# A gated mix of a state-space scan and linear attention: input loads and the order of all four engines set anew

## The chip, the cores and the metric

The kernel runs on one core of one Trainium2 chip. TensorE (PE) multiplies matrices and writes to PSUM; VectorE (DVE) and ScalarE (ACT) read PSUM and work on SBUF; GpSimd (POOL) prepares masks here; SyncE (SP) issues most of the transfers. ScalarE's and GpSimd's own queues issue some as well. The metric is the device time of one execution in microseconds (us).

## The reference, cut to what matters

```python
x = A_x                                                   # [1, 2048, 512], bf16
g = sigmoid((x * gate_w).sum(-1, keepdims=True))
# a: a diagonal complex state space of 512 states
Lam_bar = exp(dt * Lam);  B_bar = ((Lam_bar - 1) / Lam)[:, None] * Bmat
h[t] = Lam_bar * h[t-1] + x[t] @ B_bar.T
a = 2 * real(h @ Cmat.T) + x * Dskip
# b: linear attention, 32 heads of 16, with a softmax feature map of both signs
q, k, v = split(x @ wqkv)
phi(u) = concat(softmax(u @ w_phi), softmax(-u @ w_phi))
kv = sum_s phi(k)[s] v[s];  z = sum_s phi(k)[s]
b = ((phi(q) @ kv) / (phi(q) @ z + 1e-6)) @ wo
return g * a + (1 - g) * b
```

## The kernel before, in words

The 2048 rows of x are taken in four interleaved sets f = 0 to 3 (row 4r + f), each of 512. So four steps of the recurrence become one step of a scan over 512 places, and the rows between are filled in afterwards. All the work is bf16 matmuls with 128 partitions of contraction.

A function `_fast_path` does the whole computation. Behind it stands a general path, which runs only if a flag, loaded at the end, says that some value was too large for the fast one.

*Loads* (L310 to L324, L332). These are emitted ahead of everything else, so each queue issues them in program order. SP: two halves of `xn` (set 0 of x, rows on partitions, L311); three transposing loads of `xT` for sets 1 to 3 (L315); two transposing loads of `BT`, the real and imaginary parts of B (L319); `Wc` (L320); transposed `Wk` and `Wq` (L321, L322); `Wo` in four parts (L324). ScalarE's queue: `Wv` in two halves (L313), then five short vectors into `vec_n` (L317), of 1 KB each. GpSimd's queue: three short vectors in another layout into `vq` (L332). [...]

*Start.* Six matmuls on zeros (L415) come first on PE. Then PE transposes the four 128-row chunks of `xn` (L426, four 128-wide transposes each; chunks 0 and 1 need its first half, 2 and 3 its second), and ScalarE (L371) or DVE (L373) copies each from PSUM to `xT`. The V tiles (L443) are 16 units of 4 matmuls each, `Wv` being the moving operand; the first unit is a task of two matmuls (contraction parts 0 and 1, `Wv` first half) and a task of two more. Their results go to `vx` on ScalarE. The small transposes (L478, L480, L483) bring the short vectors onto partitions; after them DVE and ScalarE compute the discretised state-space parameters, which the gate, the tables for the scan and the diagonal matrices `dgL`, `dgS` and `Dd` need.

*Middle.* `g_unit` (L670, L675) multiplies x by B for each set and adds the term of the recurrence from the set before; results go to `Gs`. `scan_unit` (L708 to L726) runs the scan on DVE. `k_unit` (L782 to L813) and `q_unit` (L870) make the exponentials of the features, their sums and the state `KVbd`; `fold` (L650) multiplies `Wk` and `Wq` with `w_phi` beforehand. `fill_unit` (L750 to L758) on DVE adds the scan's carry to the sets 0, 1 and 2: its last product, L758, finishes a piece of `Gs`. The small softmax sums (L948 and around) are DVE's too.

*End.* `mix` does one block of 128 output rows at a time, 16 in all: attention numerators (L979), their evacuation (L982) and scaling (L986), the state-space output (L995, reading `Gs` and the transposed C, `CT`), a transposing transfer (L1003), the product with `Wo` added to the same PSUM bank (L1011), the evacuation with the gate's factor (L1016 on ScalarE, L1018 on DVE) and the store (L1022). The last block is evacuated and stored in two halves of 256 columns, and the flag is transposed, tested and loaded beside it.

*What sets the order.* A small planner, `_Plan` (L44 on), holds every piece of work as a task with a cost for each engine that can do it. The tuple `ORDER` (L172 on) lists all tasks in the order in which they are emitted: each entry is twice the task's number, plus one if the second of its engines takes it. Each engine so runs its tasks in the order of the list. Loads appear in the planner only as due times (`pl.at`, L378 to L379), which with the tasks' costs decide which PSUM bank a task gets: a task takes the bank that the planner thinks free first, from the groups A (four), B (two) and C (two). No due time holds an instruction up by itself; what waits on the chip are the semaphores.

Of the kernel before, what the change touches and what calls it, by code (L numbers as in the profile page):

```python
# [12 lines left out]
ACT = mybir.ActivationFunctionType  # L13
# [5 lines left out]
P = 128  # L19
# [103 lines left out]
def kernel(  # L123
# [34 lines left out]
    Pst = A_Lambda_re.shape[0]  # L158
    assert D == 512 and Pst == 512 and H * Dh == D and Dh == 16 and S == 2048
    flag_i = _fast_path(tc, A_x, A_Lambda_re, A_Lambda_im, A_B_re, A_B_im, A_C_re, A_C_im, A_log_dt, A_Dskip,  # L160
                        B_wqkv, B_w_phi, B_wo, gate_w, out)
    with tc.If(flag_i != 0, label="general"):
# [4 lines left out]
F = 4  # L167
# [2 lines left out]
GATE_LIMIT = 60.0  # L170
NWARM = 6
ORDER = (  # L172
    8, 10, 14, 18, 13, 22, 21, 156, 16, 190, 24, 266, 174, 268, 0, 26, 28, 4, 32, 162, 30, 192, 34, 158, 176, 36,
    40, 166, 2, 38, 132, 164, 42, 198, 44, 134, 46, 61, 760, 138, 53, 79, 194, 202, 196, 168, 758, 77, 55, 160,
    764, 81, 186, 67, 170, 762, 200, 182, 57, 136, 766, 154, 84, 378, 140, 172, 204, 188, 142, 144, 380, 382, 91,
    502, 178, 392, 64, 384, 63, 294, 88, 184, 286, 180, 504, 96, 288, 70, 398, 386, 282, 148, 59, 68, 73, 150,
    290, 297, 394, 292, 506, 146, 285, 388, 390, 152, 509, 75, 336, 338, 330, 298, 332, 48, 397, 404, 406, 400,
    334, 340, 83, 304, 50, 302, 86, 409, 418, 308, 306, 438, 300, 442, 444, 448, 410, 342, 344, 362, 403, 420,
    510, 346, 512, 440, 310, 348, 312, 446, 314, 450, 516, 316, 452, 422, 412, 522, 350, 352, 518, 320, 364, 454,
    354, 6, 322, 414, 424, 476, 562, 456, 514, 356, 324, 460, 462, 470, 100, 326, 98, 524, 520, 464, 416, 102,  # L180
    328, 534, 426, 526, 480, 528, 474, 358, 478, 530, 360, 466, 542, 104, 532, 472, 544, 108, 428, 546, 566, 206,
    458, 568, 548, 106, 220, 210, 430, 564, 536, 572, 482, 570, 110, 214, 318, 538, 370, 208, 372, 484, 600, 432,
    216, 574, 486, 112, 488, 212, 576, 492, 434, 226, 218, 578, 594, 494, 222, 114, 468, 496, 116, 540, 224, 238,
    228, 626, 550, 230, 498, 118, 232, 604, 234, 628, 552, 634, 246, 598, 236, 248, 580, 240, 120, 436, 602, 596,
    92, 630, 554, 250, 366, 582, 640, 252, 242, 122, 584, 586, 636, 632, 606, 556, 588, 374, 124, 768, 376, 244,
    490, 686, 642, 724, 126, 608, 500, 644, 638, 646, 726, 718, 128, 652, 590, 610, 94, 254, 728, 592, 648, 692,
    720, 368, 654, 690, 650, 696, 688, 656, 774, 658, 722, 660, 694, 666, 1210, 662, 668, 612, 270, 256, 778, 558,
    258, 1214, 780, 698, 614, 700, 702, 616, 730, 704, 670, 708, 776, 260, 618, 130, 278, 810, 710, 732, 664, 712,
    734, 620, 272, 280, 1212, 274, 798, 792, 812, 276, 672, 784, 736, 740, 674, 816, 782, 742, 802, 262, 622, 814,
    840, 624, 714, 794, 676, 716, 560, 786, 842, 744, 746, 800, 748, 834, 678, 818, 820, 804, 790, 844, 788, 796,  # L190
    808, 1204, 754, 756, 750, 828, 264, 752, 848, 846, 836, 852, 806, 850, 832, 854, 822, 856, 1208, 830, 1206,
    680, 1216, 682, 948, 944, 884, 858, 862, 864, 826, 878, 824, 838, 866, 860, 868, 946, 902, 950, 952, 880, 870,
    1062, 1036, 954, 956, 1222, 1010, 1002, 958, 706, 1220, 1076, 1218, 1004, 872, 1006, 996, 1048, 1078, 1074,
    998, 1028, 1054, 684, 1050, 960, 1056, 1012, 1000, 1052, 1030, 976, 1008, 1032, 962, 1058, 1022, 874, 1024,
    1224, 1026, 978, 964, 970, 1064, 1014, 972, 1038, 984, 1060, 1080, 1034, 980, 1226, 974, 966, 986, 982, 968,
    1184, 770, 1178, 1180, 1232, 1040, 876, 886, 1016, 1234, 1100, 882, 1082, 904, 890, 1186, 1084, 1018, 1102,
    1228, 988, 1042, 1158, 1160, 1182, 1188, 892, 1190, 894, 1086, 1114, 1152, 1230, 1154, 1066, 1068, 1106, 1156,
    1090, 1162, 1070, 1132, 1104, 1196, 990, 1192, 1092, 1072, 1164, 1094, 888, 1044, 1096, 1108, 1166, 992, 1046,
    1194, 1110, 1098, 1170, 1126, 1134, 1260, 908, 1136, 1254, 1236, 1128, 1116, 1112, 1168, 896, 1130, 738, 898,
    1198, 1172, 1262, 1280, 1238, 1118, 1138, 1264, 1200, 1256, 994, 1140, 1240, 914, 1244, 900, 906, 1020, 1312,  # L200
    1144, 1142, 1282, 1174, 1246, 1258, 916, 1314, 1248, 1306, 1120, 1286, 1268, 1266, 1272, 1146, 1308, 1288,
    1316, 1284, 1346, 1148, 1310, 1332, 1177, 918, 1338, 910, 1250, 1318, 1340, 912, 1202, 1334, 1290, 1294, 1252,
    920, 1324, 1296, 1390, 1392, 1242, 1270, 1122, 1088, 1336, 1292, 922, 926, 1342, 1274, 1384, 1276, 1386, 924,
    1320, 1364, 1358, 1298, 1360, 1322, 1151, 928, 1348, 1326, 1436, 1366, 1344, 932, 930, 1300, 1424, 1394, 938,
    1388, 940, 1302, 1328, 1362, 1350, 1410, 1125, 1396, 1352, 1442, 1416, 934, 942, 1398, 1330, 936, 1372, 1400,
    1412, 1368, 1374, 1418, 1370, 1420, 1414, 1422, 1402, 1404, 1444, 1376, 1438, 1354, 1426, 1446, 1440, 1428,
    1279, 1357, 772, 1448, 1305, 1468, 1406, 1450, 1452, 1378, 1454, 1430, 1380, 1408, 1382, 1470, 1472, 1456,
    1462, 1459, 1432, 1434, 1465, 1461, 1466)
KR = 0
GR = 0  # L210
ENGINES = {mybir.EngineType.PE, mybir.EngineType.DVE, mybir.EngineType.Activation, mybir.EngineType.Pool}
# [2 lines left out]
def _pe(n, cols):  # L214
    return {"PE": n * max(30.0, cols / 2.4 + 3.0)}
# [11 lines left out]
def _fast_path(ctx, tc, A_x, A_Lambda_re, A_Lambda_im, A_B_re, A_B_im, A_C_re, A_C_im, A_log_dt, A_Dskip,  # L227
               B_wqkv, B_w_phi, B_wo, gate_w, out):
    nc = tc.nc
    S, D, H, Dh, Pst = 2048, 512, 32, 16, 512  # L230
# [14 lines left out]
    def ctile(shape, dt, name):  # L245
        return const.tile(shape, dt, name=name)
# [10 lines left out]
    Wv = ctile([P, KT, D], BF16, "Wv")  # L257
# [29 lines left out]
    vec_n = ctile([20, P], BF16, "vec_n")  # L287
# [10 lines left out]
    xn = wk.tile([P, F, D], BF16, tag="ET0", name="xn", bufs=1)  # L298
# [8 lines left out]
    nc.scalar.preload_act_table_set(ACT_SET)  # L307
    vsrc = (A_log_dt, A_Lambda_re, A_Lambda_im, A_Dskip, gate_w)
    x0 = xf[0].rearrange("(a c) d -> c a d", c=P)
    for h in range(2):  # L310
        nc.sync.dma_start(out=xn[:, 2 * h:2 * h + 2], in_=x0[:, 2 * h:2 * h + 2])  # L311
    for k in (0, 2):
        nc.scalar.dma_start(out=Wv[:, k:k + 2, :], in_=B_wqkv[k * P:(k + 2) * P, 2 * D:3 * D].rearrange("(k p) n -> p k n", p=P))  # L313
    for f in range(1, F):
        nc.sync.dma_start_transpose(out=xT[:, :, f * NCH:(f + 1) * NCH], in_=xf[f])  # L315
    for n, src in enumerate(vsrc):
        nc.scalar.dma_start(out=vec_n[4 * n:4 * n + 4, :], in_=src.rearrange("(j p) -> j p", p=P))  # L317
    for ri, B_ in enumerate((A_B_re, A_B_im)):
        nc.sync.dma_start_transpose(out=BT[:, :, ri, :], in_=B_)  # L319
    nc.sync.dma_start(out=Wc[:], in_=B_w_phi.rearrange("(k hl) e f -> (hl e) k f", hl=8))  # L320
    nc.sync.dma_start_transpose(out=WkT, in_=B_wqkv[:, D:2 * D])  # L321
    nc.sync.dma_start_transpose(out=WqT, in_=B_wqkv[:, 0:D])  # L322
# [7 lines left out]
    nc.gpsimd.memset(KVbd[:], 0.0)  # L330
    for n in range(3):
        nc.gpsimd.dma_start(out=vq[:, n, :], in_=vsrc[n].rearrange("(q t) -> q t", t=2 * NT))  # L332
    nc.vector.memset(eps_t[:], 1e-6)
    nc.vector.memset(hpi_t[:], float(np.pi / 2.0))
    nc.vector.memset(sg[0:64, :], 1.0)
# [3 lines left out]
    nc.vector.memset(selq[:], 0.0)  # L339
    nc.vector.memset(vx[:, :, :, Dh:Dh + 1], 1.0)  # L340

    pl = _Plan({"DVE": 2.4e3, "ACT": 5.0e3, "PE": 1.1e3, "SP": 26.0e3})

    def psum(prefix):
        def make(k):
# [28 lines left out]
        return pl.add(cost, fn, deps=deps, bufs=[b] + list(bufs), rank=rank)  # L374

    A1 = ("A", "B")
    d_x = [pl.at(t) for t in (4.1, 4.9, 7.7, 10.2, 12.7)]
    d_wv0, d_wv, d_b, d_wk, d_wq, d_wo = (pl.at(t) for t in (4.9, 5.7, 18.0, 21.0, 23.3, 26.0))  # L378
    d_vec, d_wc = pl.at(8.5), pl.at(18.5)  # L379

    def tcols(f, a):
        return slice(f * NCH + a * P, f * NCH + (a + 1) * P)
# [38 lines left out]
    for a in range(4):  # L421
# [5 lines left out]
        t = pl.add({"PE": 460.0} if a < 2 else _pe(4, 128), tr, deps=[d_x[a // 2]], follow=[t_warm], bufs=[b, early[0]])  # L427
# [1249 lines left out]
```

## Time and profile before

Device time in four runs: 154.40, 154.03, 154.10 and 153.65 us, median 154.07.

| | |
|---|---|
| profiled execution, its own time | 154.53 us |
| its span | 152.4 us |
| mean granted clock of PE | 0.993 |
| busy: PE, DVE, ACT, POOL | 145.1, 129.1, 110.1, 4.3 us |
| PE matmuls | 1124 |
| moved by the DMA engines | 14.95 MB, 98 GB/s in the mean |
| landings: `xn` halves, `Wv` halves | 4.11, 5.57; 4.67, 6.19 us |
| landings: `xT` sets 1, 2, 3; `BT` | 9.62, 10.47, 13.84; 16.0, 17.9 us |

Times inside the execution count from the start of its span. In the profile, a row of slices gives the busy share of each fortieth of the span in tenths. A row of the timeline gives the start, the length, the engine (PEld is PE's weight load, SPq, ACTq and POOLq are queues of transfers), the line of the kernel, the operation, what it writes and reads, the shape, how many instructions stand in the row, and in brackets how long the engine had been idle before and what ended that.

### The profile page before, as it was taken

The page shows a single profiled execution, that of the slowest core. Times are in us where ns is not written, and L with a number is a line of the kernel's source. Part 1 is how long each engine was busy: PE and PEld are TensorE (multiplying, and loading weights), DVE is VectorE, ACT ScalarE, POOL GpSimd, SP SyncE. Part 2 cuts the span into 40 slices and gives each one's busy share as a digit, 9 for nine tenths or more (in the row PEclk, how much of TensorE's full clock was granted, in tenths as well). Part 3 has the DMA queues.
Part 4 walks back from the last instruction along what each step waited for, and adds up shares of the span by engine and source line. Part 5 has one row for each costly group of instructions (what it writes and reads, how often), then busy time and mean ns, then how long its engine had stood idle before and what let it go on. Part 6 is the DMA issues. An engine that isn't in the chain of part 4 may idle for free.

```text
span 152.4 us, 3179 instructions
## 1 busy us (share of the span) xinstructions
PE 145.1 (95%) x1124; PEld 83.8 (55%) x1124; DVE 129.1 (85%) x370; ACT 110.1 (72%) x221; POOL 4.3 (3%) x14
## 2 busy tenths in 40 slices
PE   6899999999999999999999999999999999999950
PEld 1535566555566656655545565756555556555720
DVE  2407999799999999999799999999999999998030
ACT  3217898998888898989999999877784756263130
POOL 8200000000000000000000000000000000000000
PEclk9999999999999999999999999999999999999997
DMA  3969998900112323434133213033744141227330
GB/s 112 312 144 271 171 210 210 234 8 0 34 34 69 73 69 103 106 89 52 34 86 103 97 49 103 22 69 69 73 105 104 35 103 39 69 69 201 77 92 24
DMA packets 37211, 14.95 MB, mean 98 GB/s; under 512 B 29384, under 2 KB 37192, under 8 KB 37192
## 3 DMA queue, kind: packets, MB, share of 16 engines
q1 hardware_dynamic: 35504, 13.33, 39.9%
q10 hardware_dynamic: 1592, 1.38, 2.8%
q8 instruction: 10, 0.16, 0.5%
q14 instruction: 9, 0.07, 0.2%
q0 software_dynamic: 96, 0.00, 0.0%
HBM read 1.60 MB, written 2.10 MB: 24 GB/s over the span
## 4 chain that ended last, share of the span: by engine, by line


## 5 line engine op out<-in xcount | busy, mean ns | idle before, releaser
L670 PE MATMUL pp<-xT,BT 128*128 128x512 bf16 x128 | 32.0, 380 | 0.0
L995 PE MATMUL pp<-CT,Gs 128*128 128x512 bf16 (+1 forms) x104 | 23.7, 363 | 0.0
L670 PEld LDWEIGHTS <-BT 128*128 128x128 bf16 x128 | 17.8, 145 | 8.9
L982 ACT CAST late<-pp 128x512 bf16<-128x512 f32 x32 | 17.9, 589 | 5.8 <-PE pp L979 5.8
L1016 ACT ACTIVATE late<-pp,Gg 128x512 bf16<-128x512 f32 x15 | 10.3, 691 | 13.6 <-PE pp L1011 10.9
L240 ACT ACTIVATE E<-pp 128x512 bf16<-128x512 f32 x32 | 17.6, 606 | 1.3 <-PE pp L782 0.6
L240 ACT ACTIVATE ET<-pp 128x512 bf16<-128x512 f32 x32 | 17.3, 617 | 0.7 <-PE pp L870 0.6
L443 PE MATMUL pp<-Wv,xT 128*128 128x512 bf16 x64 | 17.3, 416 | 0.0
L1011 PE MATMUL pp<-Wo,late 128*128 128x512 bf16 (+1 forms) x68 | 16.1, 366 | 0.0
L782 PE MATMUL pp<-Wk,xT 128*128 128x512 bf16 x64 | 15.6, 379 | 0.0
L870 PE MATMUL pp<-xT,Wq 128*128 128x512 bf16 x64 | 15.4, 379 | 0.0
L995 PEld LDWEIGHTS <-Gs 128*128 128x128 bf16 x104 | 9.6, 98 | 7.5
L986 DVE TENSOR_TENSOR late<-late 128x512 bf16<-128x512 bf16 x32 | 13.0, 434 | 0.0
L371 ACT CAST Gs<-pp 128x512 bf16<-128x512 f32 x20 | 11.7, 591 | 1.6 <-PE pp L675 1.6
L371 ACT CAST vx<-pp 128x512 bf16<-128x512 f32 x16 | 8.8, 602 | 4.4 <-PE pp L443 4.3
L979 PE MATMUL pp<-KVbd,ET 128*128 128x128 bf16 x128 | 10.7, 219 | 0.1
L443 PEld LDWEIGHTS <-xT 128*128 128x128 bf16 x64 | 6.5, 107 | 7.8 <-issue 2.4
L979 PEld LDWEIGHTS <-ET 128*128 128x128 bf16 x128 | 8.5, 98 | 3.4 <-DVE qmax L949 0.3
L782 PEld LDWEIGHTS <-xT 128*128 128x128 bf16 x64 | 6.2, 98 | 6.8
L806 DVE TENSOR_TENSOR E<-E,rc 128x2048 bf16<-128x2048 bf16 x8 | 9.6, 1221 | 0.0
L870 PEld LDWEIGHTS <-Wq 128*128 128x128 bf16 x64 | 6.0, 98 | 6.6
L718 DVE TENSOR_TENSOR_SCAN c<-sp,c 128x512 bf16<-128x512 f32 x8 | 9.4, 1216 | 0.0
(170 smaller groups left out, 242.4 us busy)
## 6 DMA issues: line engine op xcount, KB each, us to landing
Zs<-c SPq DMA_DIRECT2D x32, 64.0 KB, 2.1
out_dram<-late SPq DMA_DIRECT2D x9, 128.0 KB, 2.1
c<-c SPq DMA_DIRECT2D x16, 64.0 KB, 2.0
CT<-ET SPq DMA_DIRECT2D x8, 128.0 KB, 3.1
out_dram<-late ACTq DMA_DIRECT2D x6, 128.0 KB, 1.9
xn<-in_A_x_dram SPq DMA_DIRECT2D x2, 256.0 KB
Wv<-in_B_wqkv_dram ACTq DMA_DIRECT2D x2, 256.0 KB, 4.9
Wo<-in_B_wo_dram SPq DMA_DIRECT2D x4, 128.0 KB, 2.8
```

Source lines behind the costliest of these rows:

```text
L240: return nc.scalar.activation(**kw)
L371: nc.scalar.copy(out=o, in_=view(b))
L443: MM(out=f32v(b), lhsT=xT[:, kt, tcols(f, a)], rhs=Wv[:, kt, :], start=(kt == 0), stop=(kt == KT - 1))
L670: MM(out=f32v(b), lhsT=BT[:, kt].rearrange("p r (q t) -> p (r q) t", t=NT)[:, :, j + 4 * h], rhs=xT[:, kt, f * NCH:(f + 1) * NCH], start=( ...
L782: MM(out=f32v(b), lhsT=xT[:, kt, tcols(f, a)], rhs=Wk2[:, kt, :], start=(kt == 0), stop=(kt == KT - 1))
L870: MM(out=f32v(b), lhsT=Wq2[:, kt, g * P:(g + 1) * P], rhs=xT[:, kt, f * NCH:(f + 1) * NCH], start=(kt == 0), stop=(kt == KT - 1))
L979: MM(out=f32v(pn[sgn])[:, g * P:(g + 1) * P], lhsT=ets[f].t[:, sgn, g, cs], rhs=KVbd[:, sgn, g, :], start=True, stop=True)
L982: tn = pl.add(_act(512), lambda e, sgn=sgn: nc.scalar.copy(out=o2.t[:, sgn], in_=f32v(pn[sgn])), deps=[t], bufs=[pn[sgn], o2], rank=rank + 2)
L986: VT(out=v, in0=v, in1=als[f].t[:, a, sgn * H:(sgn + 1) * H].rearrange("p (g h) -> p g h", g=HG).unsqueeze(2).to_broadcast([P, HG, Dh, 8]) ...
L995: MM(out=f32v(py)[:, 0:w], lhsT=st, rhs=CT[:, tt // 2 + 4 * (tt % 2), n * w:n * w + w], start=(tt == 0), stop=False)
L1011: MM(out=f32v(py)[:, 0:w], lhsT=oT.t[:, g, :], rhs=Wo[:, g, hs], start=False, stop=(g == HG - 1))
L1016: nc.scalar.mul(out=ot.t[:, hs], in_=f32v(py)[:, 0:w], mul=Gg[:, ti:ti + 1])
```

## The change

The loads are emitted in another order. The second half of `Wv` moves from ScalarE's queue to SP, between the halves of `xn`; the third `xT` moves behind both parts of `BT`; the fourth and fifth short vectors of `vec_n` move from ScalarE's to GpSimd's queue, behind `vq`. The due times are written anew, and the whole of `ORDER` is replaced, for all engines. The shapes and the number of PE's instructions stay as they are. Some tasks go to the other engine: `Gs` evacuations on DVE are 6 in place of 4 (18 on ScalarE in place of 20), those of `Wk` 1 in place of 2, those of `xT` 3 in place of 2. On PE the list now begins with the warm-up matmuls, the transposes of chunks 0 and 1, the first two matmuls of V (entry 156), the transposes of chunks 2 and 3 (18 and 22), and then the rest of V; before, entry 156 stood behind 22. After V of set 0 and the small transposes, V tiles of sets 1 and 2 and three of the gate's units come ahead of the work on `BT`, and what reads the third set of x comes at the 27th PE task or later.

```diff
 ORDER = (
-    8, 10, 14, 18, 13, 22, 21, 156, 16, 190, 24, 266, 174, 268, 0, 26, 28, 4, 32, 162, 30, 192, 34, 158, 176, 36,
...
+    8, 10, 13, 14, 156, 18, 17, 22, 2, 174, 158, 20, 25, 266, 160, 4, 190, 0, 26, 28, 270, 194, 192, 30, 32, 176,
...
-    for h in range(2):
-        nc.sync.dma_start(out=xn[:, 2 * h:2 * h + 2], in_=x0[:, 2 * h:2 * h + 2])
-    for k in (0, 2):
-        nc.scalar.dma_start(out=Wv[:, k:k + 2, :], in_=B_wqkv[k * P:(k + 2) * P, 2 * D:3 * D].rearrange("(k p) n -> p k n", p=P))
-    for f in range(1, F):
+    nc.sync.dma_start(out=xn[:, 0:2], in_=x0[:, 0:2])
+    for k, q in ((0, nc.scalar), (2, nc.sync)):
+        q.dma_start(out=Wv[:, k:k + 2, :], in_=B_wqkv[k * P:(k + 2) * P, 2 * D:3 * D].rearrange("(k p) n -> p k n", p=P))
+    nc.sync.dma_start(out=xn[:, 2:4], in_=x0[:, 2:4])
+
+    def xload(f):
         nc.sync.dma_start_transpose(out=xT[:, :, f * NCH:(f + 1) * NCH], in_=xf[f])
-    for n, src in enumerate(vsrc):
-        nc.scalar.dma_start(out=vec_n[4 * n:4 * n + 4, :], in_=src.rearrange("(j p) -> j p", p=P))
+    xload(1)
+    xload(2)
     for ri, B_ in enumerate((A_B_re, A_B_im)):
         nc.sync.dma_start_transpose(out=BT[:, :, ri, :], in_=B_)
+    for n in range(3):
+        nc.scalar.dma_start(out=vec_n[4 * n:4 * n + 4, :], in_=vsrc[n].rearrange("(j p) -> j p", p=P))
+    xload(3)
...
     for n in range(3):
         nc.gpsimd.dma_start(out=vq[:, n, :], in_=vsrc[n].rearrange("(q t) -> q t", t=2 * NT))
+    for n in range(3, 5):
+        nc.gpsimd.dma_start(out=vec_n[4 * n:4 * n + 4, :], in_=vsrc[n].rearrange("(j p) -> j p", p=P))
...
-    pl = _Plan({"DVE": 2.4e3, "ACT": 5.0e3, "PE": 1.1e3, "SP": 26.0e3})
+    pl = _Plan({"DVE": 2.4e3, "ACT": 5.6e3, "PE": 1.1e3, "SP": 27.0e3})
...
-    d_x = [pl.at(t) for t in (4.1, 4.9, 7.7, 10.2, 12.7)]
-    d_wv0, d_wv, d_b, d_wk, d_wq, d_wo = (pl.at(t) for t in (4.9, 5.7, 18.0, 21.0, 23.3, 26.0))
-    d_vec, d_wc = pl.at(8.5), pl.at(18.5)
+    d_x = [pl.at(t) for t in (4.1, 6.2, 9.2, 11.4, 19.5)]
+    d_wv0, d_wv, d_b, d_wk, d_wq, d_wo = (pl.at(t) for t in (4.8, 5.6, 17.0, 22.7, 24.8, 27.0))
+    d_vec, d_wc = pl.at(9.5), pl.at(20.5)
```

## The prediction

> **What bounds the kernel now.** I read the page's busy shares first, then its slices, then busy time by stretches, then the order of time at the start, then the waits.
>
> ```profile
> PE 145.1 (95%) x1124; PEld 83.8 (55%) x1124; DVE 129.1 (85%) x370; ACT 110.1 (72%) x221; POOL 4.3 (3%) x14
> PE   6899999999999999999999999999999999999950
> DVE  2407999799999999999799999999999999998030
> ```
>
> TensorE (PE) is the bound: 145.1 of 152.4 us. Its slices are full from the third to the 38th. VectorE (DVE) is nearly as full from the fourth on, and the average of 85% hides this: what it lacks lies in the first 12 us and the last 12.
>
> ```profile
> 4.20:6.40 2.20, 1.78 (x16) 1.52 (x17) 0.56 (x2) 0.17 (x1) 0.75 (x2) 1.00 1.16 332
> 6.40:11.50 5.10, 5.10 (x17) 1.85 (x14) 0.79 (x7) 1.50 (x3) 0.00 (x0) 1.00 0.81 172
> ...
> 30.00:70.00 40.00, 40.00 (x266) 24.07 (x265) 39.64 (x102) 35.94 (x75) 0.00 (x0) 1.00 0.27 63
> 70.00:100.00 30.00, 29.88 (x288) 17.11 (x286) 28.91 (x71) 28.24 (x63) 0.00 (x0) 1.00 0.21 64
> 100.00:140.00 40.00, 40.00 (x330) 22.99 (x327) 39.90 (x114) 24.60 (x48) 0.00 (x0) 1.00 0.40 83
> 140.00:152.40 12.40, 7.02 (x54) 4.34 (x51) 1.86 (x9) 2.07 (x3) 0.00 (x0) 0.92 0.31 79
> ```
>
> After each stretch come its length and the busy time of PE, weight loads, DVE, ACT and POOL (instructions in brackets), then granted clock, DMA share and GB/s. From 30 to 140 us PE is busy 109.88 of 110 us: no matmul there can start earlier unless one before it does. So only about 11 us at the start and 5 at the end can give time back. DVE is busy 39.90 of the 40 us before 140, so in that stretch every microsecond of DVE work added or started late comes out somewhere.
>
> ```profile
> 1.27 2.74 PE L415 MATMUL pp<-warm 128*128 128x512 bf16 x6 [1.27 <-DVE warm L306]
> ...
> 4.16 1.03 PE L426 MATMUL pp<-ident,xn 128*128 128x128 bf16 x8
> ...
> 5.61 1.04 PE L426 MATMUL pp<-ident,xn 128*128 128x128 bf16 x8 [0.42 <-DMA xn<-in_A_x_dram]
> ...
> 6.44 5.17 PE L443 MATMUL pp<-Wv,xT 128*128 128x512 bf16 x14
> ...
> 11.55 0.18 PE L478 MATMUL pp<-ident,vec_n 20*128 20x20 bf16 x1
> ```
>
> Columns: start, length, engine, line. Four transposes of x need a chunk of `xn` each; the second half of `xn` landed at 5.57, so PE stood from about 5.0 to 5.61. The 14 matmuls of V began at 6.44. They start 0.427 us apart until 10.45, and 0.216 apart afterwards: the clock was low for the first ten.
>
> ```profile
> ACT xT L371 <- PE pp L426: 4.1, 1, 4.1
> ACT vx L371 <- PE pp L443: 3.5, 1, 3.5
> ```
>
> [...]
>
> **The change, part by part.** (1) *First two V matmuls into the gap.* Each of the two input issues on SP took 0.49 us (0.98 for two, from 0.74). The order on SP becomes `xn` first half at 0.74, `Wv` second half at 1.23, `xn` second half at 1.72, with `Wv` first half on ScalarE's queue at 0.86 as before. The four 256 KB loads landed at 4.11, 4.67, 5.57 and 6.19 in the order of their issue; the second half of `xn` goes from third to fourth, so I take 6.19 for it (ends: 5.57, if queues share the engines so that its place is kept; 6.5, if it comes behind more of SP's work). PE then does: transposes 4.16 to 5.0; the first evacuation, 4.81 to 5.23 in the row of DVE; two V matmuls from about 5.30, 2 x 0.427 = 0.85, to 6.15; transposes from 6.23 (landing plus 0.04, as 5.57 to 5.61) to 7.06 (8 x 0.107, less the overlap at the end). Before, the transposes ended at 6.44; two V matmuls after them ended at 7.29. So the same work is done at 7.06 instead of 7.29: 0.23 us gained at the low clock. If the clock rises at the same moment, 0.23 us of work at 0.427 per matmul is worth 0.23 x 0.216 / 0.427 = 0.12 us. With the ends of the landing: +0.4 (there the idle gap is only 0.3) to -0.15.
>
> (2) *The clock.* [...] The trace shows the low spacing from 1.27 to 10.45, 9.2 us, although PE was busy most of it: the last 3.41 us (7.04 to 10.45) were the first such stretch with PE busy throughout; in the 3.44 us before, it was busy 2.88, or 84%. [...] I take the row, and keep +0.3 and -1.7 for the range.
>
> (3) *Loads in another order.* [...] From the rows, a transposing issue holds SP 1.8 to 2.6 us: `xT` 1 and 2 at about 10 and 10.5, `BT` about 14 (16.0 and 17.9 before), third `xT` about 16 (13.8 before), `Wk` about 20.3 (22.0). The first matmul to read `BT` comes about 19, the third `xT` about 24.6, `Wk` about 25, so each is covered by 3 us or more: zero. Without the cover, each us late would be a us of PE. The fourth and fifth `vec_n` go to POOL behind three `vq` issues (3.33 to 4.95), two more of 0.50: issued by 5.95, landing 4.7 to 5.0 later like `vq`, by 10.9; the small transposes (L478) that read them come at 11.55 or later: zero now, up to 0.8 if the clock rose early. ScalarE gets free of two issues, and evacuates from about 5 us on: no gain by itself, since PE's next wait is for `xn`.
>
> (4) *The new order.* PE's instructions are the same 1124; none is removed. Some evacuations change sides: DVE gets two more of `Gs` (2 x 0.686, L373), one more `xT` (0.425) and one diagonal more, gives back one of `Wk` (0.688), and takes one 512-wide half of the last output in place of 256. In the stretch where DVE is full this is about 0.95 us more. Before, DVE idled 9.40 - 8.06 + 40.00 - 39.64 + 30.00 - 28.91 + 0.10 = 2.9 us from 20.6 to 140, but 1.3 of it before 30, where little work is ready. The readiest measure is how long before an L995 matmul the last L758 product it reads was done: 0.37, 0.62 and 0.95 us at the tightest three fills, 0.33 at the small softmax sums. Adding the work of PE and DVE in the two orders by the durations of these rows, the tightest fill is 2.15 us of PE work behind its DVE work after, 2.28 before; so the margin of 0.62 would go to about 0.5, and PE would not wait: zero, with 0.95 + 0.5 (DVE's main work starts at the small transposes, and those are two V matmuls' time later at the worst) - 0.4 = 1.1 us as the upper end. No gain is possible there, since PE is full.
>
> (5) *The end.* The last output block is split between ACT and DVE in halves as before; last matmul to last store issue is 1.245 us in the trace, and the flag's transpose, its load and its test stay beside it: zero, +-0.1.
>
> **Sum.** Profiled execution: 154.53 us, of which the span is 152.4. 154.53 - 0.12 (1, 2) + 0 (3, 4, 5) = 154.41, span 152.3. The profiled execution lies 0.46 above the median 154.07, which gives 153.95, say 153.9.
>
> **Rivals.** [...] *(b) DVE becomes the bound of the middle.* For it: 39.90 of 40, margins of 0.3 to 0.6, 0.95 us more work; against: the added-up margins hardly move. Place: L995 matmuls waiting for L758 products, or the small softmax sums (L948). It decides from 0.4 us of lag on; a lag of 0.95 to 1.45 gives 154.07 + 0.6 to 1.1 = 154.7 to 155.2, and with a second such place 155.6. [...]
>
> **How the numbers follow.** What a measurement can tell from no change is about 0.3%, 0.46 us. Forecast (0.35 in all): 153.9, own range 153.4 to 154.3; 0.12 of it is faster than 153.61. (a) 0.20, faster. (b) 0.28, slower but for 0.03. (c) 0.11, of which 0.09 slower. (d) 0.06, the same. Faster 0.12 + 0.20 = 0.32; slower 0.25 + 0.09 = 0.34; same 0.34. The range leaves out the best of (a) and the worst of (b): 152.5 to 155.4.
>
> **What would show it.** Right: two V matmuls between the two pairs of transposes, starting about 5.3; the last pair from 6.2; spacing of 0.427 until about 10.4; no idle PE between 12 and 146; no hole in the DMA row at 10 us; L478 not waiting for a DMA. (a) shows as spacing 0.216 from 7 or 8 us on; (b) as idle time ahead of L995 or L979 with DVE as its releaser, and PE under 39.9 in the stretch from 100 to 140; (c) as transposes at 6.5 or later. The prediction is wrong if PE, which has the same work, has more than 0.5 us more or less of idle and slow time than 7.3 us.

## The result, and the profile after

| | before | after |
|---|---|---|
| median of the executions | 154.03 us (55) | 153.82 us (34) |
| ratio, 95% interval | | 1.0008 (0.9992 to 1.0025) |
| profiled execution, its own time | 154.53 us | 155.52 us |
| its span | 152.4 us | 153.6 us |

No difference can be told: 153.9 was forecast. But the changed kernel's executions lie in two heaps. Of 36 listed with their span, 26 lie between 153.2 and 154.2 us and 10 between 155.1 and 155.7, with nothing between. The profiled one is of the upper heap, so its trace must not be read as the changed kernel's usual course. The kernel before has one heap. Executions more than 1.5% above the quickest of their kernel are left out of the ratios and of the figures of experiments 2 (158.34, 159.80) and 10 (156.75); 155.69 here and 156.00 and 156.09 in experiment 1 are such too, and the upper heap stands without them.

The page of the changed kernel, busy shares and slices:

```profile
PE 145.3 (95%) x1124; PEld 83.5 (54%) x1124; DVE 131.1 (85%) x373; ACT 108.3 (70%) x218; POOL 5.3 (3%) x16
...
PE   6899999999999999999999999999999999999930
...
DVE  2336999979999999997999999999999999999120
```

PE's work is the same; DVE has 131.1 us in place of 129.1. The stretches, in the columns explained above:

```profile
4.20:6.40 2.20, 1.94 (x10) 0.90 (x10) 1.02 (x4) 0.00 (x0) 1.78 (x4) 1.00 1.16 314
...
70.00:100.00 30.00, 29.66 (x288) 17.03 (x287) 28.63 (x70) 27.21 (x61) 0.00 (x0) 1.00 0.30 79
100.00:140.00 40.00, 39.93 (x324) 22.92 (x323) 39.83 (x109) 24.87 (x49) 0.00 (x0) 1.00 0.44 77
140.00:153.60 13.60, 7.48 (x56) 4.57 (x53) 3.51 (x13) 1.85 (x3) 0.00 (x0) 0.88 0.32 82
```

PE is busy 0.29 us less than before between 70 and 140, and the last stretch is 1.2 us longer. The start of the same execution, PE's rows (`x` transposes are L432 now, V L449, the small transposes L484):

```profile
4.37 1.03 PE L432 MATMUL pp<-ident,xn 128*128 128x128 bf16 x8 [0.35 <-DMA xn<-in_A_x_dram]
...
5.50 1.03 PE L449 MATMUL pp<-Wv,xT 128*128 128x512 bf16 x2
...
6.45 1.04 PE L432 MATMUL pp<-ident,xn 128*128 128x128 bf16 x8
...
7.28 4.71 PE L449 MATMUL pp<-Wv,xT 128*128 128x512 bf16 x14
...
11.91 0.18 PE L484 MATMUL pp<-ident,vec_n 20*128 20x20 bf16 x1
```

Two V matmuls stand in the gap, as the order says; the second half of `xn` landed at about 6.4. The matmuls start 0.427 us apart until 10.26, as in the kernel before. (The column of the granted clock reads 1.00 in these first stretches of both kernels all the same. In experiment 3 the same spacing, 0.427, stands beside a granted clock of 0.54; so at the start I take the spacing as the sign of the clock.) The small transposes come 0.36 later than before, at 11.91, but after 16 V matmuls instead of 14. At 0.216 each, PE is there 0.07 us ahead.

PE's weight loads waited for DVE, which the profile before did not show at these lines (waits of the changed kernel: total, times, longest):

```profile
PEld L1001 <- DVE Gs L764: 0.8, 2, 0.5
```

In this execution, in which the clock rises late, the last matmul starts at 147.20 instead of 146.74, 0.46 later, and from there to the end of the span it takes 6.42 us instead of 5.68, 0.74 more. The sum is the 1.2 us between the spans.

### The profile page after: what moved, and what is told of

It is laid out like the page before. It is cut to its first block, busy times and chain, and to the rows that moved or that the text cites. A ratio compares the mean times of both kernels' runs of the same rounds, so it can differ in the third digit from the quotient of the medians.

```text
span 153.6 us, 3168 instructions
## 1 busy us (share of the span) xinstructions
PE 145.3 (95%) x1124; PEld 83.5 (54%) x1124; DVE 131.1 (85%) x373; ACT 108.3 (70%) x218; POOL 5.3 (3%) x16
## 4 chain that ended last, share of the span: by engine, by line
PE 44%; DVE 39%; SPq 5%; DMA 4%; issue 3%; ACT 2%; DVEq 0%; ACTq 0%
PE pp L1001 9%; PE pp L676 9%; PE pp L449 8%; PE pp L788 6%; PE pp L1017 5%; DVE c L724 5%; DVE late L992 4%; DVE c L760 3%; DVE E L812 3%; DVE c L756 3%; DVE c L757 3%; SPq L744 3%; DMA xn<-in_A_x_dram 2%; DVE st L805 2%; DVE ET L604 2%
## 5 line engine op out<-in xcount | busy, mean ns | idle before, releaser
L676 PE MATMUL pp<-xT,BT 128*128 128x512 bf16 x128 | 31.3, 381 | 0.0
L1001 PE MATMUL pp<-CT,Gs 128*128 128x512 bf16 (+1 forms) x104 | 23.7, 363 | 0.1
L449 PE MATMUL pp<-Wv,xT 128*128 128x512 bf16 x64 | 17.2, 415 | 0.1
L1022 ACT ACTIVATE late<-pp,Gg 128x512 bf16<-128x512 f32 (+1 forms) x15 | 10.0, 679 | 10.0 <-PE pp L1017 7.0
L876 PE MATMUL pp<-xT,Wq 128*128 128x512 bf16 x64 | 14.9, 379 | 0.0
L1001 PEld LDWEIGHTS <-Gs 128*128 128x128 bf16 x104 | 9.5, 98 | 8.0 <-DVE Gs L764 0.8
L992 DVE TENSOR_TENSOR late<-late 128x512 bf16<-128x512 bf16 x32 | 12.9, 430 | 0.0
L377 ACT CAST Gs<-pp 128x512 bf16<-128x512 f32 x18 | 10.3, 599 | 3.4 <-PE pp L676 2.0
L985 PE MATMUL pp<-KVbd,ET 128*128 128x128 bf16 x128 | 11.3, 219 | 0.0
L449 PEld LDWEIGHTS <-xT 128*128 128x128 bf16 x64 | 6.4, 105 | 7.7 <-issue 1.9
```

Of the source, the lines that this page charges most:

```text
L377: nc.scalar.copy(out=o, in_=view(b))
L449: MM(out=f32v(b), lhsT=xT[:, kt, tcols(f, a)], rhs=Wv[:, kt, :], start=(kt == 0), stop=(kt == KT - 1))
L676: MM(out=f32v(b), lhsT=BT[:, kt].rearrange("p r (q t) -> p (r q) t", t=NT)[:, :, j + 4 * h], rhs=xT[:, kt, f * NCH:(f + 1) * NCH], start=( ...
L876: MM(out=f32v(b), lhsT=Wq2[:, kt, g * P:(g + 1) * P], rhs=xT[:, kt, f * NCH:(f + 1) * NCH], start=(kt == 0), stop=(kt == KT - 1))
L985: MM(out=f32v(pn[sgn])[:, g * P:(g + 1) * P], lhsT=ets[f].t[:, sgn, g, cs], rhs=KVbd[:, sgn, g, :], start=True, stop=True)
L992: VT(out=v, in0=v, in1=als[f].t[:, a, sgn * H:(sgn + 1) * H].rearrange("p (g h) -> p g h", g=HG).unsqueeze(2).to_broadcast([P, HG, Dh, 8]) ...
```

## Experiments

**1. The changed kernel again.** No edit.

> The changed kernel once more, unedited. Its 36 executions so far lie in two heaps, 26 near 153.7 us and 10 near 155.4 us, with nothing between 154.2 and 155.1; the profiled one (155.52) is of the upper heap. [...] Theory B (transfers): the heaps differ by late landings, of x's second half or of the last store; then the clock rises at the same time in both and the 1.7 us are in the start's gaps or behind the last matmul. About one execution in four falls near 155.4 either way.

Twelve executions: six between 153.66 and 154.33, six between 155.51 and 156.09. The profiled one took 154.14, and its PE rows are:

```profile
4.45 0.62 PE L432 MATMUL pp<-ident,xn 128*128 128x128 bf16 x8 [0.43 <-DMA xn<-in_A_x_dram]
5.36 0.61 PE L449 MATMUL pp<-Wv,xT 128*128 128x512 bf16 x2 [0.30 <-DVE xT L379]
6.64 0.62 PE L432 MATMUL pp<-ident,xn 128*128 128x128 bf16 x8 [0.67 <-DMA xn<-in_A_x_dram]
7.09 3.19 PE L449 MATMUL pp<-Wv,xT 128*128 128x512 bf16 x14
10.21 0.18 PE L484 MATMUL pp<-ident,vec_n 20*128 20x20 bf16 x1
```

The eight transposes take 0.62 us by the row instead of 1.03, and 14 V matmuls 3.19 instead of 4.71: the clock was high from 4.45 on. The small transposes come 1.70 us earlier than in the other heap (10.21 against 11.91), the distance of the heaps. The transfers were no earlier here (the second transposes start at 6.64, when `xn` ends PE's wait, and at 6.45 in the other), so the heap is the clock's. The end differs little: 6.50 us from the last matmul's start to the end, against 6.42. The last matmul starts at 145.86. This is 1.34 earlier than with the late clock: 0.36 of the 1.70 is given back, as PE now waits before L1001 near 95, 109 and 121 us, and not only near 96 and 122 (experiments 8 and 9 and step 4 of the next part show why).

**2. Loads alone, and 3. order alone.** The first is the kernel before with the new load lines, the second the changed kernel with the old ones:

```diff
 loads_only, against the kernel before (the other load lines as in the change):
-    for h in range(2):
-        nc.sync.dma_start(out=xn[:, 2 * h:2 * h + 2], in_=x0[:, 2 * h:2 * h + 2])
...
+    nc.sync.dma_start(out=xn[:, 0:2], in_=x0[:, 0:2])
+    for k, q in ((0, nc.scalar), (2, nc.sync)):
...
+    xload(3)
 order_only, against the changed kernel: the same lines the other way round
```

> The kernel before, with the new order of loads alone (its old ORDER and due times). Second half of x lands at about 6.4 instead of 5.57, and no matmul of V stands before it, so the idle gap of PE at the start is 1.3 us instead of 0.6, and V starts at about 7.3 instead of 6.44. [...] Theory B': the order of the middle is what costs, and the loads are free: 154.0 to 154.4.

> The changed kernel with the old order of loads (new ORDER and due times kept). Second half of x lands at 5.57 again, two V matmuls still fill the gap. Theory A: the gap is about 0.3 us and ends before 6.2 us; the heap with the late clock gets smaller or vanishes, 153.5 to 153.8 for most. Theory B': if the new order of the middle costs (PE waits for DVE of about 0.36 us more were in the profile), it is hidden in both kernels alike and the time is 154.3 or more in every execution with a late clock. [...]

Measured: 155.64 and 156.68 us for the loads alone, 1.1 and 2.2 above the median of the kernel before beside them, 154.50, so that the sign can be told but not the size; 159.48 for the order alone (ratio 1.0337, 1.0280 to 1.0394). Both are slower than either whole; for the order alone neither theory had that. The parts belong together. With the loads alone, PE stands 1.6 us after the matmul at 16.5, for `xT`, whose third set the old order reads early and the new loads bring late. With the order alone PE waits for what the old loads bring late (PE's waits from 5 to 22 us of `order_only`, lines as in before):

```profile
PE pp L670 <- DMA BT<-in_A_B_im_dram: 3.4, 1, 3.4
```

The first matmul on `BT` stood until 20.79, and the spacing after it is 0.427 again: the clock had fallen (granted clock 0.54 from 20.8 to 26). Before that, the short vectors were late as well:

```profile
5.64 0.61 PE L426 MATMUL pp<-ident,xn 128*128 128x128 bf16 x8
6.08 3.19 PE L443 MATMUL pp<-Wv,xT 128*128 128x512 bf16 x14
9.99 0.17 PE L478 MATMUL pp<-ident,vec_n 20*128 20x20 bf16 x1 [0.72 <-DMA vec_n<-in_A_Dskip_dram]
```

The second half of `xn` did come earlier here, V started at 6.08, and nothing came of it.

**4. The gap filled with idle matmuls, changed kernel.**

```diff
-NWARM = 6
+NWARM = 7
         def tr(e, b=b, a=a):
+            if a == 2:
+                MM(out=f32v(b)[:, 0:P], lhsT=warm[:, 0:P], rhs=warm[:, 0:P], start=True, stop=True)
...
             def fn(e):
+                if ti == 0 and k0 == 0:
+                    MM(out=f32v(b), lhsT=warm[:, 0:P], rhs=warm[:], start=True, stop=True)
```

> The changed kernel with three idle matmuls on zeros more, which change no result: a seventh warm-up, one of 512 columns just before the first two V matmuls, one of 128 just before the third transpose. They fill PE's idle time from 4.0 to 4.37, from 5.1 to 5.5 and at 6.4 and delay the rest by at most 0.2 us. [...] Theory B: the heaps stay as they are, near 153.8 and 155.5, in the same shares.

One heap is left: 20 executions between 153.61 and 154.53, median 154.17, where 16 of 48 listed executions without the edit lay above 155.1. The ratio to the kernel before is 0.9976 (0.9963 to 0.9989). So with less idle time of PE at the start the clock rises early in every execution, by their heap, where it did in two of three. Which of the three fillers does it was not separated, and PE still stood 0.51 us for `xn` at 6.51 in the profile. It did not get below the lower heap: the early clock is all that there is to win there.

**5. The same for the kernel before.**

```diff
-NWARM = 6
+NWARM = 7
         def tr(e, b=b, a=a):
+            if a == 2:
+                for w_ in (512, 128):
+                    MM(out=f32v(b)[:, 0:w_], lhsT=warm[:, 0:P], rhs=warm[:, 0:w_], start=True, stop=True)
```

> The kernel before with a seventh warm-up matmul and two idle ones on zeros (512 and 128 columns) ahead of the third transpose; they fill PE's idle time from 4.0 to 4.16 and 5.0 to 5.6 and change no result. [...] Rival: the new loads are what lets the early clock be used (vec_n, third xT); then PE waits early, for xT or the short vectors, and 154.0 or more.

154.51 us, ratio 1.0023 (1.0006 to 1.0041): no gain, and the rival is right. The clock was high by 4.2 us; the first V matmul starts at 5.90 in place of 6.44 and the matmuls are 0.216 apart. But the last matmul starts at 146.65, against 146.74. PE's waits from 5 to 22 us in it:

```profile
PE pp L673 <- ACT vx L371: 1.2, 1, 1.2
PE pp L481 <- DMA vec_n<-in_A_Dskip_dram: 0.9, 1, 0.9
```

L481 are the small transposes, L673 the first matmul on `BT` (20.76, against 20.87 in the kernel before). The profile of experiment 6, also of the kernel before in all but the flag and by chance with an early clock, puts the second wait to the load:

```profile
PE pp L670 <- DMA BT<-in_A_B_im_dram: 1.1, 1, 1.1
PE pp L478 <- DMA vec_n<-in_A_Dskip_dram: 0.9, 1, 0.9
```

There PE began it at 20.95. The table ahead of the prediction has 17.9 for this landing (18.02 by the last step of the transfer's semaphore). In the four profiles with the old loads and an early clock (`order_only`, 5, 6 and 10) that last step comes at 20.45 to 20.82, and PE begins between 20.58 and 20.95: the landing itself is 2.4 to 2.8 us later there. In all four at most 15 packets end between 17.5 and 18.0, where 169 do in the kernel before; what holds them, and whether that is all of the delay, the traces do not tell. In the kernel before, then, an early clock is eaten up by the old loads, which accounts for its one heap: its own profile has the late clock and that of experiment 6 the early one, and their last matmuls start 0.10 us apart. In the changed kernel `vec_n` and `BT` come early enough for it to be used.

**6. The flag late, kernel before.** One entry of the order moved:

```diff
-    ... 1408, 1382, 1470, 1472, 1456, 1462, ...
+    ... 1408, 1382, 1456, 1470, 1472, 1462, ...
```

> The kernel before with one entry of ORDER moved: the flag's transpose and test stand between the two halves of the last output block instead of ahead of them, as in the changed kernel. Theory T (the end): GpSimd's branch on the flag comes 0.45 us later, the 16 KB instruction load that follows it by 1.3 us starts 0.45 later and still shares an engine with the last store, whose last packets wait for its end; 154.5 to 154.9 beside 154.1 to 154.5 for the kernel before, 0.3 to 0.6 slower, and the last matmul comes at the same time. Rival: the late end of the changed kernel comes from its stores' queues (two of the last four on ScalarE's); then no difference.

154.77 us, ratio 1.0027 (1.0015 to 1.0040), 0.42 us. The last matmul starts 0.10 later than in the profile of the kernel before (146.84), the span's end comes 6.29 us after it in place of 5.68. So moving the flag behind the first half block is worth most of the 0.74 by which the changed kernel ends later. DMA issues and landings at the end, of the kernel before (size, us to landing):

```profile
out_dram<-late SPq DMA_DIRECT2D x1, 64.0 KB, 2.9
```

and of the changed kernel:

```profile
out_dram<-late SPq DMA_DIRECT2D x1, 64.0 KB, 3.5
```

This is the last store of 256 columns, and the span waits for it. In the traces' packets, one load of 16 KB of program runs from 148.45 to 149.83 in the kernel before, from 149.29 to 150.71 in the changed one, from 148.93 to 150.53 here. Each time most of the store's packets are through 0.4 to 0.5 us after its first, and the last ones only after that load's end (150.28, 151.16, 150.98), by 0.45 us in each of the three. Three or four loads of 8 KB run there as well, but the last of those ends 0.4, 0.9 and 1.0 us ahead of the store, so it is not they. In the kernel before and here nine packets are left over; they start at 149.81 and 150.53, as the load ends. Nine is a sixteenth of the store's 144, and the page counts 16 DMA engines: by this estimate it is the share of one of them. The load starts 1.23 to 1.29 us after PE's branch on the flag (147.16, 148.06, 147.70); GpSimd's is 0.04 ahead of it, so which of the two asks for it isn't told apart.

**7. The flag early, changed kernel; 8. with the gap filled; 9. the second once more; 10. kernel before with both.** The flag's transpose and test go right behind their preparation on DVE:

```diff
-    ... 1380, 1468, 1404, 1454, 1452, 1407, 1409, 1456,
-    1470, 1472, 1458, 1462, 1465, 1382, 1466, 1461)
+    ... 1380, 1468, 1470, 1472, 1404, 1454, 1452, 1407, 1409, 1456,
+    1458, 1462, 1465, 1382, 1466, 1461)
```

> The changed kernel with the flag's transpose and test at the early place, and no idle matmuls: the flag's edit without that of the clock. Theory: the two heaps of the changed kernel stay (late clock in a quarter to a half of the executions) and both move down by what the end gives, 0.7 to 1.5 us: near 152.3 and 154.1. If after_fill_flag owed its 2.1 us to something else than the end, the lower heap stays above 153.2.

> after_fill with the flag's transpose and test moved ahead of the last blocks, right behind the flag's own preparation on DVE, some 3 us earlier. Theory T: the 16 KB load is over before the last store starts, which then lands in 1.2 us as the half store on ScalarE's queue did, instead of 2.8: 152.6 to 153.3, some 1.0 to 1.5 below after_fill; the last matmul comes at the same time. Rival: the tail is set by the engines' other instruction loads or by the store itself: same as after_fill within 0.3.

> after_fill_flag once more, unedited. Its four executions gave 152.07, its profiled one had the last matmul 0.73 us earlier than after_fill, although the order up to 140 us is the same: there, the load of 16 KB of program at 94.81 was over before the last piece of Zs came; in after_fill it began at 95.64, and held the last five packets of Zs until 97.0, and DVE waited 0.83 us (L761). If that is chance of the execution, some of the executions now lie 0.5 to 0.8 higher, near 152.7; if not, all lie within 151.9 to 152.4.

> before_fill with the flag's transpose and test moved to the same early place. Both theories together: below before_fill by 0.8 to 1.3 (the collision costs the kernel before about 0.6 less than the changed one): 151.5 to 152.6. If the moved transpose makes PE wait for DVE, up to 0.5 of it is lost.

| kernel | median us | ratio to before (95%) | last matmul's start | from there to the end |
|---|---|---|---|---|
| changed, flag early | 151.80 | 0.9853 (0.9821 to 0.9884) | 145.17 | 4.60 |
| changed, filled | 154.17 | 0.9976 (0.9963 to 0.9989) | 145.86 | 6.49 |
| changed, filled, flag early | 152.07 | 0.9860 (0.9836 to 0.9883) | 145.13 | 5.05 |
| the same again | 152.16 | 0.9878 (0.9848 to 0.9909) | 145.57 | 4.58 |
| before, filled | 154.51 | 1.0023 (1.0006 to 1.0041) | 146.65 | 5.52 |
| before, filled, flag early | 154.34 | 1.0003 (0.9981 to 1.0025) | 146.48 | 5.60 |

Moving two entries of the changed kernel's order takes it to 151.80 us, 1.5% under the kernel before and the lowest median of all. Its last store, in the same view:

```profile
out_dram<-late SPq DMA_DIRECT2D x1, 64.0 KB, 1.9
```

The program load ran from 145.83 to 146.78 and the store's packets from 146.88 to 147.49, one behind the other. All four executions of `after_flag` were quick (151.56 to 151.98), so the upper heap that was expected at 154.1 did not show; four are too few to say that it is gone.

In the kernel before, the same move brought nothing, a miss. There the 16 KB load came at 147.72, in the middle of the last store (issued at 147.32, last packet over at 150.09), 1.24 after the last matmul's start where it was 0.66 in `after_flag`. Eight packets of each of the last four stores ran only from 148.65, the load's end, to 150.09; the first of them had been due since about 146.6, before the load, and what held them until then is not told. With the flag early the branch of PE (it starts at 144.3 to 144.8 in the four profiles) no longer sets the load's start, and what does is open. So the collision is shown, and that an early flag can avoid it; that it always does is not.

The executions of experiments 8 and 9 lie between 151.88 and 152.45, nearer together than was expected, and lower than the 152.6 to 153.3 that was expected of experiment 8: its last matmul came 0.73 us earlier than that of `after_fill`, which the flag was not to change. Their profiles show what did it, and that it differs between executions. DVE's rows of `after_fill`:

```profile
96.98 0.35 DVE L760 TENSOR_SCALAR c<-Zs,sp 128x512 bf16<-128x512 bf16 x1
98.05 0.35 DVE L761 TENSOR_SCALAR c<-Zs,sp 128x512 bf16<-128x512 bf16 x1 [0.72 <-DMA Zs<-c]
```

and of `after_fill_flag`, in which DVE ran level with it up to here:

```profile
96.94 0.34 DVE L760 TENSOR_SCALAR c<-Zs,sp 128x512 bf16<-128x512 bf16 x1
97.22 0.35 DVE L761 TENSOR_SCALAR c<-Zs,sp 128x512 bf16<-128x512 bf16 x1
```

In the first, another load of 16 KB of program ran from 95.64 to 96.57, and the last 5 of a `Zs` transfer's 80 packets went from 96.56 to 97.03; in the second it ran from 94.81 to 95.74, and they were over by 96.20. What DVE waited here, PE lost at two fills that follow (the pauses ahead of the mix's matmuls on `Gs`, L995 in the kernel before, near 109 and 120 us: from one matmul's start to the next, less the usual 0.216 us):

| early clock, profile of | DVE waited for `Zs` | PE lost at the two fills |
|---|---|---|
| `fill_flag_wvact` (12) | 0.75 | 0.37 + 0.25 |
| `after_fill` | 0.72 | 0.37 + 0.25 |
| `after_again` | 0.6 | 0.31 + 0.25 |
| `after_fill_flag2` | 0.42 | 0.13 + 0.25 |
| `after_fill_flag`, `after_flag` | 0 | 0 |

So DVE has no more than 0.15 us to spare there, both fills together, and the last matmul's start in the table before moves with it (145.13 and 145.17 without the wait, 145.57 and 145.86 with it).

**11. Less work on DVE, changed kernel filled.** One L754 addition of a fill is left out, so part of a carry term is missing:

```diff
         def f2(e):
+            if (j, f) == (0, 1):
+                return
             VT(out=b1.t[:], in0=b1.t[:], in1=b2.t[:], op=ALU.add)
```

> after_fill without one addition on DVE (L758 in the kernel before counts the last product; this is the one before it, L754, of one of the twelve fills, about 0.60 us at 100.4 us), so that the kernel leaves out part of one set's carry term: its time tells what DVE's lag costs. Theory DVE: the two waits of PE for fills that come after it in after_fill, 0.37 us at 109.2 and 0.25 at 120.7, vanish or nearly so; the last matmul comes 0.5 to 0.6 earlier, 153.6 in place of 154.17. Rival: PE waits there for a bank or for ScalarE, DVE's record only being the last: less than 0.2 us.

153.57 us (20 executions), ratio 0.9959 (0.9945 to 0.9974), where `after_fill` had 0.9976 (0.9963 to 0.9989) in another set. The difference of the ratios is 0.26 us, and their intervals overlap. In the profile PE's two losses are gone, but in this profile `Zs` was not held either, which alone takes them away by the table. The run is inconclusive for what the addition costs.

**12. Wv back on ScalarE's queue, changed kernel filled with the flag early.**

```diff
-    for k, q in ((0, nc.scalar), (2, nc.sync)):
+    for k, q in ((0, nc.scalar), (2, nc.scalar)):
```

> after_fill_flag with the second half of Wv back on ScalarE's queue: one part of the change undone. Then x's second half is the second transfer on SP again and lands at about 5.6 to 5.9 instead of 6.4, and Wv's second half at 6.2. The third transpose starts as soon as the V matmuls in the gap end, about 5.9 to 6.3, and the rest of V up to 0.5 earlier at the start, with the early clock: 0 to 0.5 us faster than after_fill_flag, 151.6 to 152.1. Rival: the transfers share the engines, so that x's second half lands at 6.3 as well: same within 0.2.

152.01 us against 152.16 and 152.07: the same. The third transpose starts at 5.59 instead of 6.5 and V is done 0.9 earlier, but the small transposes come at 9.98 instead of 10.06 to 10.13, because PE stood 0.71 us for `vec_n` there: this is where the early V ends. So `Wv` in halves on two queues neither wins nor loses anything that four executions can tell, once the clock is early.

## Why the prediction was right or wrong

The time was right, and the reasons for it only in part: two terms put at zero, the clock and the end, were each above 0.7 us and of opposite sign in the usual execution, and a third, the new order, was 0.3 to 0.9. That they cancel was luck. The prediction's own sign of being wrong came true in the profiled execution: PE's idle time is 8.3 us (153.6 - 145.3), more than 0.5 off the 7.3 that it named.

1. **V matmuls into the gap**, +0.23 us at the low clock, 0.12 in all: confirmed with the late clock. They stand there; `xn` landed at 6.4 instead of 6.19, inside the ends given (5.57 to 6.5), and PE is 0.07 us ahead of before at the same count of V matmuls.
2. **The clock**, "I take the row": this step failed for most executions. In about two in three (32 of 48 listed ones, by their heap) the clock rose by 6.5 us, not at 10.4. The rise lies between 4.0 and 6.5 in eleven profiled executions and near 10.4 in three, never between. The early rise is worth 1.70 us at the small transposes. One profiled execution of the kernel before could not tell this. An earlier rise, (a) among the chances, was given 0.20, and came. That the clock stayed low through a stretch filled to 84% was no measure against it: in the kernel before PE was busy for all of the 4.84 us from 5.61 to 10.45, and V's matmuls were 0.427 us apart to the end of it, so the last 3.41 us were not the first such stretch. And in experiment 1 the clock was up at 4.45, after the 2.74 us of the warm-up (1.28 to 4.02) and a pause of 0.43. What sets the moment of the rise no run shows beyond experiment 4; the same instructions gave both. Nor does any run show the terms of +0.3 and -1.7 that the range keeps as they were reckoned; in their place the runs showed no rise later than about 10.4, and the 1.70 us above for an early one.
3. **Loads, zero:** right as far as it went: no wait of PE for them in the changed kernel, although they landed about 1 us later than worked out (`BT` at 15.2, third `xT` at 17.2 with the late clock, in place of 14 and 16). The hole in the DMA row at 10 us is gone: in the kernel before the third `xT`'s issue waited 1.8 us on SP for an `xT` transfer, began at 9.63, as the first `xT` landed (9.62), and no packet moved from 10.02 to 10.93; in the changed kernel SP's issues waited for no load up to 20 us, and the DMA engines moved no less than 110 GB/s in any 0.2 us from 6 to 14. ScalarE's first evacuation came at 6.23 in the kernel before, 0.04 after the end of its last `vec_n` issue, and at 7.09 in the changed one, when PE's transposes were done, not from 5 us on. What the step missed is that they are the price of admission for step 2: with the old loads the early clock gains nothing (experiment 5).
4. **The new order, zero:** "PE would not wait" failed. Near 95 us PE stands 0.34 us in every profile of the new order, 0.12 in the kernel before. The wait is for the maximum on DVE that frees a PSUM bank of the small softmax sums. In the kernel before it follows its sum at once:

```profile
95.21 0.42 DVE L948 TENSOR_TENSOR q<-pp,q 128x256 f32<-128x256 f32 x1
95.54 0.42 DVE L949 TENSOR_REDUCE qmax<-pp 128x1 f32<-128x256 f32 x1
```

In the changed kernel two other pieces, of L992 and L957, stand between:

```profile
95.57 0.42 DVE L954 TENSOR_TENSOR q<-pp,q 128x256 f32<-128x256 f32 x1
...
96.44 0.42 DVE L955 TENSOR_REDUCE qmax<-pp 128x1 f32<-128x256 f32 x1
```

PE's wait for it:

```profile
PE pp L1001 <- DVE qmax L955: 0.3, 1, 0.3
```

At the fills PE loses 0.23 with the late clock, and with the early one 0 to 0.62, as far as `Zs` is held. That is rival (b)'s place; against the kernel before it makes 0.3 to 0.9 us from the start to the last matmul, below or at the lower part of the lag that (b) assumed. The margin of 0.5 us that was worked out for the tightest fill was 0.15 at most with the early clock, and a late transfer, which the sum of DVE's work did not hold, uses it up. That DVE's 0.95 us of added work is the cause was not settled by experiment 11, and the stretches speak against it: from 30 to 140 us DVE is busy 107.0 us in the changed kernel and 108.5 before. By the rows above it is the order of the work at 95 us and not its amount; no run put L955 back behind L954.
5. **The end, zero, +-0.1:** failed: 0.74 us with the late clock, 0.82 with the early one. "The flag's transpose, its load and its test stay beside it" counted the engines' time and missed the load of 16 KB of program that comes 1.23 to 1.29 us behind the flag's branch (experiment 6), and at whose end the store's last packets went. The transpose came 0.48 us before the last matmul's start instead of 0.92, and the load followed it.

The balance with the early clock, against the profiled kernel before: last matmul 0.88 us earlier (145.86), end 0.82 later, -0.07 of the span. With the late clock: +0.46 and +0.74. The lower heap lies near 153.7 us and the upper near 155.4, against 154.0 before; two thirds of the one and a third of the other give a mean of about 154.2, which is the tie of the ratio, 1.0008. The median alone, 153.82, is the lower heap's. The sum of the prediction came near it because it left out a gain and losses of like size.

## What to carry to other kernels

Where a run's times lie in heaps, find out which heap the profile is of before reading it, and profile the other. A faster start is worth what the next waits leave of it: ask which load or engine would be waited for then. And look in the packets for a load of program behind a branch at the end of a kernel (here 16 KB, 1.23 to 1.29 us after it): try the branch where that load meets no store, and look again whether it did.

## What the runs showed of the hardware that was not expected

- Loads of 16 KB of program, ten in an execution of 150 us, each 0.9 to 1.8 us long. Where one met a transfer, the transfer's last packets came late: 5 of 80 of `Zs` were over at 97.03 in `after_fill`, the load ending at 96.57, and by 96.20 in `after_fill_flag`, where it ended at 95.74; of the final store's 144, 135 were through by 149.18 in the kernel before and the other 9 went from 149.81 to 150.28, the load ending at 149.83; in the changed kernel the last 27 went from 149.94 to 151.16, 12 of them after the load's end at 150.71. By my estimate, from 80 / 16 and 144 / 16, these are the shares of one to three of the 16 DMA engines that the page counts.
- PE's clock rose after 2.7 to 5.2 us from the first warm-up matmul or not until about 9.1, and both with the same instructions (`after` and `after_again`; the kernel before and experiment 6).
- After PE had stood 3.4 us for `BT` (experiment 3), the matmuls were 0.427 us apart again, and the granted clock read 0.54.
- With an early clock and the old loads the second half of `BT` landed at 20.45 to 20.82 us, and at 18.02 with a late one (experiment 5); the cause is open.
